# One attention-and-MLP decode kernel: w2 in five pieces, biases by one product each, and six unread products around the second norm

## The chip, the cores and the metric

The kernel runs on one core of one Trainium2 chip. The metric is the device time of one execution in microseconds (us). Lower is better. Three executions of the kernel before are at hand, and a fourth that was taken with the hardware profiler.

## What is computed

Eight tokens (B = 8, one position each, D = 512) go through one transformer block with modulation from a condition `c`. All numbers are float32.

```python
mod = (silu(c) @ w_mod).reshape(8, 6, 1, 512)
sa, ca, ga, sb, cb, gb = (mod[:, i] for i in range(6))
h = layernorm(x) * (1 + ca) + sa
x = x + ga * attention(h)          # 32 query heads, 8 cached heads, last 2048 of 8192 positions
h = layernorm(x) * (1 + cb) + sb
u = h @ w1 + b1                    # w1: 512 x 1792
x = x + gb * (relu(u) ** 2 @ w2 + b2)   # w2: 1792 x 512
```

The cached keys and values in the window and all weights are read from device memory once: 165 MB.

## The kernel before, in words

**Loads.** All large loads go out on SP's queue in the order of the list `loads`: `w_mod` and `wq` in two parts each, then keys and values of the eight tokens in turn, then `wo`, `w1` and `w2`. They share four buffers of 4 MB, `slot0` to `slot3`; `done()` frees a buffer behind its last reader and `pump()` issues the next load. `load()` (line 81) cuts the last ones into pieces, so that products can start on a piece while the next is on its way: `wo` in four, `w1` in three (two of its four row blocks, then one, then one), and `w2` like this:

```python
cuts = ((0, 8), (8, 11), (11, 12), (12, 13))
pieces = [(lo, v[:, lo:hi]) for lo, hi in cuts]
```

A unit of these cuts is one row of `w2` on each of 128 partitions, 256 KB, 13 in all (`FC`). The 128 rows of `w2` that are left over, the "extra" rows, go to the tile `w2x`, which lies in the memory of `qb_all`, in two small loads ahead of these (line 108). The tile framework gives each load on a hardware queue one of eight semaphores in turn, so a load also waits until the load eight places ahead of it has landed.

**Layout.** A row vector of 512 is spread over the partitions in four groups of 32, of which eight are in use, with 128 columns each. Most products have 32 columns of the array as target (`32 * q : 32 * q + 32`), and four of them stand side by side. In the profile a float32 product is two MATMUL records and two LDWEIGHTS records.

**The end of the program**, which the change touches, is a chain through all engines:

1. The attention's output times `wo` on PE (lines 472 to 497), then gate and residual on DVE (498, 499); the latter also leaves the row sums `x1sum`.
2. The second layer norm, `norm()` (line 170): PE sums `x1sum` over the groups with `sel` (line 173), DVE makes the mean, ACT squares the difference and sums it (line 178), PE sums that (line 182), ACT takes the root (184), DVE scales, shifts and transposes to `h2T` (188 to 192, 157).
3. `h2T` times `w1` on PE: the bias `b1` is put into the sum by products with a piece of the identity, one for each of four groups (line 509) and two for the extra columns (513); then for each of four row blocks `kc` two products for the extra columns into `px` (522) and four for the main columns into `ph` (530).
4. ACT takes the relu of `px` (539) and of `ph` in two halves (548, 551); DVE squares and transposes each to `rxT` and `rT` (549 to 554).
5. The product with `w2` on PE: four products for `b2` (558), then 17 chunks of four products (565): first the four of the extra rows (`rxT`, `w2x`), then the thirteen of the main rows (`rT`, `w2t`), in order. Each main chunk needs its piece of `w2`.
6. DVE applies gate and residual (573, 574), and SP stores the result.

PE works through its instructions in program order, and so do ACT and DVE.

Of the kernel before, what the change touches and what calls it, by code (L numbers as in the profile page):

```python
# [8 lines left out]
F32 = mybir.dt.float32  # L9
AF = mybir.ActivationFunctionType  # L10
# [8 lines left out]
def tile_adaln_cached_attention_mlp(  # L19
# [14 lines left out]
    nc = tc.nc  # L34
    P = 128
    B, HKV, SK, DH = k_cache.shape
    D = wq.shape[0]
# [27 lines left out]
    b1_x = consts.tile([1, FX], F32, name="b1_x")  # L65
    b2_in = consts.tile([NQ, P], F32, name="b2_in")
    nc.scalar.dma_start(b1_in, b1[: P * FC].rearrange("(g n) -> g n", g=NQ))
    nc.scalar.dma_start(b1_x, b1[P * FC :].rearrange("(g n) -> g n", g=1))
    nc.gpsimd.dma_start(b2_in, b2.rearrange("(g n) -> g n", g=NQ))


# [9 lines left out]
    def load(key):  # L81
        s = free.pop(0)
        t = slots[s]
        held[key] = s
        kind = key[0]
        if kind in "KV":

            src = k_cache if kind == "K" else v_cache
            v = src[key[1], 4 * key[2] : 4 * key[2] + 4, SK - W :, :]
            v = v.rearrange("x (i j) d -> i x (j d)", i=32)  # L90
            nc.sync.dma_start(t, v)
            return
        if kind == "mod":
            pieces = [(0, w_mod.rearrange(r_kc, p=P)[:, 2 * key[1] : 2 * key[1] + 2])]
        elif kind == "wq":
            pieces = [(0, wq.rearrange(r_kc, p=P)[:, 2 * key[1] : 2 * key[1] + 2])]
        elif kind == "wo":
            v = wo.rearrange("(p i) n -> p i n", p=P)
            cuts = ((0, 16),) if key[1] == 0 else ((16, 24), (24, 28), (28, 32))
            pieces = [(lo - 16 * key[1], v[:, lo:hi]) for lo, hi in cuts]  # L100
        elif kind == "w1":
            v = w1.rearrange(r_kc, p=P)
            pieces = [(lo, v[:, lo:hi]) for lo, hi in ((0, 2), (2, 3), (3, 4))]
        else:

            for g, o, first, _ in EXTRA:
                v = w2[first : first + 16 * o].rearrange("(i o c) n -> o i (c n)", i=4, o=o)
                nc.sync.dma_start(w2x[g : g + 4 * o, :], v)
            v = w2[: P * FC].rearrange("(p c) n -> p c n", p=P)
            cuts = ((0, 8), (8, 11), (11, 12), (12, 13))  # L110
            pieces = [(lo, v[:, lo:hi]) for lo, hi in cuts]
        for lo, v in pieces:
            a, n = v.shape[1:]
            nc.sync.dma_start(t[:, lo * n : (lo + a) * n].rearrange("p (a n) -> p a n", n=n), v)
# [52 lines left out]
    def bank(name="m_ps"):  # L167
        return ps_m.tile([P, 512], F32, name=name, tag="m_ps")

    def norm(xt, rowsum):  # L170

        pa = bank()
        nc.tensor.matmul(pa[:, 0:1], sel, rowsum, start=True, stop=True)  # L173
        nmean = work.tile([P, 1], F32, name="nmean")
        nc.vector.tensor_scalar(nmean, pa[:, 0:1], -1.0 / D, None, op0=ALU.mult)
        sq = work.tile([P, P], F32, name="sq", bufs=1)
        ssq = work.tile([P, 1], F32, name="ssq")
        nc.scalar.activation(sq, xt, AF.Square, bias=nmean, scale=1.0, accum_out=ssq)
        xm = work.tile([P, P], F32, name="xm", bufs=1)
        nc.vector.tensor_scalar(xm, xt, nmean, None, op0=ALU.add)  # L180
        pb = bank()
        nc.tensor.matmul(pb[:, 0:1], sel, ssq, start=True, stop=True)
        rstd = work.tile([P, 1], F32, name="rstd")
        nc.scalar.activation(rstd, pb[:, 0:1], AF.Sqrt, bias=eps, scale=1.0 / D)
        return xm, rstd
# [285 lines left out]
    for i in range(28):  # L471
        nc.tensor.matmul(  # L472
            wo_ps[32 * (i % 4) : 32 * (i % 4) + 32, :],
            oT[:, i, :],
            slot(("wo", i // 16), D)[:, i % 16, :],
            start=(i < 4),
            stop=(i >= 24),
        )
    x1 = consts.tile([P, P], F32, name="x1")
    x1sum = work.tile([P, 1], F32, name="x1sum")  # L480
    at_i = work.tile([P, D], F32, name="at_i", tag="a")
# [15 lines left out]
            )  # L497
    nc.vector.tensor_mul(x1, pw[:, :P], mods[0][:, 2, :])
    nc.vector.scalar_tensor_tensor(x1, x1, 1.0, x_in, op0=ALU.mult, op1=ALU.add, accum_out=x1sum)
    xm, rstd = norm(x1, x1sum)  # L500
    nc.vector.tensor_mul(xm, xm, mods[1][:, 1, :])
    h2T = scaled(xm, rstd, mods[1][:, 0, :], "h2T")

    w1t = slot(("w1",), F)
    w2t = slot(("w2",), D)
    ph = ps_t.tile([P, 512], F32, name="t_ps")
    px = bank()
    for g in range(NQ):
        nc.tensor.matmul(
            ph[32 * g : 32 * g + 32, :FG], one[:NQ, g : g + 1].to_broadcast([NQ, 32]), b1_in, start=True, stop=False  # L510
        )
    for g, o, _, at_ in EXTRA:
        nc.tensor.matmul(
            px[g : g + 32, : 16 * o],
            one[:1, :1].to_broadcast([1, 32]),
            b1_x[:, at_ : at_ + 16 * o],
            start=True,
            stop=False,
        )
    for kc in range(NQ):  # L520
        for g, o, first, _ in EXTRA:
            nc.tensor.matmul(
                px[g : g + 32, : 16 * o],
                h2T[:, kc, :],
                w1t[:, kc, first : first + 16 * o],
                start=False,
                stop=(kc == NQ - 1),
            )
        for g in range(NQ):
            nc.tensor.matmul(  # L530
                ph[32 * g : 32 * g + 32, :FG],
                h2T[:, kc, :],
                w1t[:, kc, g * FG : (g + 1) * FG],
                start=False,
                stop=(kc == NQ - 1),
            )

    for g, o, _, _ in EXTRA:
        nc.scalar.activation(
            rx[g : g + 32, : 4 * o, :].rearrange("p (o i) c -> p i o c", i=4),  # L540
            px[g : g + 32, : 16 * o].rearrange("p (i o c) -> p i o c", i=4, o=o),
            AF.Relu,
        )
    r = work.tile([P, 32, FC], F32, name="relu", tag="a")
    rT = work.tile([P, FC, 32], F32, name="rT", bufs=1)
    rxT = work.tile([64, 4, 32], F32, name="rxT", bufs=1)
    h = ph[:, :FG].rearrange("p (l c) -> p l c", l=32)
    nc.scalar.activation(r[:, :, :6], h[:, :, :6], AF.Relu)
    nc.vector.tensor_mul(rx, rx, rx)
    nc.vector.transpose(rxT, rx.rearrange("p l c -> p c l"))  # L550
    nc.scalar.activation(r[:, :, 6:], h[:, :, 6:], AF.Relu)
    for lo, hi in ((0, 6), (6, FC)):
        nc.vector.tensor_mul(r[:, :, lo:hi], r[:, :, lo:hi], r[:, :, lo:hi])
        nc.vector.transpose(rT[:, lo:hi], r[:, :, lo:hi].rearrange("p l c -> p c l"))

    py = ps_t.tile([P, 512], F32, name="t_ps")
    for q in range(NQ):
        nc.tensor.matmul(
            py[32 * q : 32 * q + 32, :P], one[:NQ, q : q + 1].to_broadcast([NQ, 32]), b2_in, start=True, stop=False
        )  # L560
    chunks = [(rxT[:, c, :], w2x[:64, D * c : D * c + D]) for c in range(4)]
    chunks += [(rT[:, f, :], w2t[:, f, :]) for f in range(FC)]
    for f, (left, right) in enumerate(chunks):
        for q in range(NQ):
            nc.tensor.matmul(  # L565
# [46 lines left out]
```

## Time and profile before

| | |
|---|---|
| three executions | 391.80, 391.89, 392.67 us; median 391.89 us |
| the profiled execution | 392.46 us, of which its span is 390.7 us |
| busy shares of the span | PE 66%, DVE 55%, PE's weight loads 30%, ACT 11%, GpSimd (POOL) 2% |
| moved by the DMA engines | 165.05 MB, mean 422 GB/s over the span |
| the chain that ended last | DMA 55%, DVE 24%, PE 20% of the span |

The profile is of one execution. Times in it are counted from the start of its span. "Granted clock" (PEclk) is the share of full speed that the chip granted to PE's clock: 1.0 is 2.4 GHz, 0.5 is 1.2 GHz. "DMA share" is the mean busy share of the 16 DMA engines; in short stretches it can read over 1.

### The profile page before, as it was taken

The page shows a single profiled execution, that of the slowest core. Times are in us where ns is not written, and L with a number is a line of the kernel's source. Part 1 is how long each engine was busy: PE and PEld are TensorE (multiplying, and loading weights), DVE is VectorE, ACT ScalarE, POOL GpSimd, SP SyncE. Part 2 cuts the span into 40 slices and gives each one's busy share as a digit, 9 for nine tenths or more (in the row PEclk, how much of TensorE's full clock was granted, in tenths as well). Part 3 has the DMA queues.
Part 4 walks back from the last instruction along what each step waited for, and adds up shares of the span by engine and source line. Part 5 has one row for each costly group of instructions (what it writes and reads, how often), then busy time and mean ns, then how long its engine had stood idle before and what let it go on. Part 6 is the DMA issues. An engine that isn't in the chain of part 4 may idle for free.

```text
span 390.7 us, 4952 instructions
## 1 busy us (share of the span) xinstructions
PE 257.5 (66%) x2196; PEld 116.3 (30%) x2196; DVE 214.3 (55%) x231; ACT 42.4 (11%) x90; POOL 6.1 (2%) x13
## 2 busy tenths in 40 slices
PE   0282808678966693859485939394849485984975
PEld 0120301151341342223322523143324323352344
DVE  3420299399394939284928491939293937330031
ACT  0310100030030003001200120003000300140010
POOL 4000000000000000000000000000000000100000
PEclk9997768969976998778688977786889777898788
DMA  8999999999999999999999999999999999999994
GB/s 325 435 429 434 436 429 450 433 439 429 428 429 428 429 428 429 429 438 440 429 433 431 436 441 433 429 431 429 428 429 429 435 433 428 433 438 414 428 427 166
DMA packets 7079, 165.05 MB, mean 422 GB/s; under 512 B 841, under 2 KB 1010, under 8 KB 1650
## 3 DMA queue, kind: packets, MB, share of 16 engines
q1 hardware_dynamic: 6952, 164.70, 98.1%
q8 instruction: 17, 0.28, 0.3%
q10 hardware_dynamic: 74, 0.04, 0.0%
q14 instruction: 4, 0.03, 0.0%
q0 software_dynamic: 32, 0.00, 0.0%
HBM read 164.67 MB, written 0.07 MB: 422 GB/s over the span
## 4 chain that ended last, share of the span: by engine, by line
DMA 55%; DVE 24%; PE 20%; issue 1%; ACT 0%; SPq 0%; DVEq 0%; ACTq 0%
DMA slot<-in_A_k_cache_dram 34%; DVE slot L304 22%; PE s_ps L314 16%; DMA slot<-in_A_wq_dram 7%; DMA slot<-in_A_wo_dram 6%; DMA slot<-in_B_w_dram 5%; DMA slot<-in_w_mod_dram 3%; PE t_ps L260 2%; PE t_ps L565 1%; PE m_ps L275 1%; PE t_ps L385 1%; DVE pT L386 0%; PE o_ps L397 0%; ACT qrep L283 0%; ACT prd L375 0%
## 5 line engine op out<-in xcount | busy, mean ns | idle before, releaser
L304 DVE STREAM_TRANSPOSE slot<-slot 128x2048 f32<-128x2048 f32 x64 | 143.8, 2282 | 41.7 <-DMA slot<-in_A_k_cache_dram 41.7
L314 PE MATMUL s_ps<-slot,qb_all 128*32 128x512 f32 x512 | 121.7, 1098 | 67.9 <-DVE slot L304 67.5
L314 PEld LDWEIGHTS s_ps<-slot,qb_all 128*32 128x32 f32 x512 | 22.6, 136 | 146.2 <-issue 80.8
L397 PE MATMUL o_ps<-slot,pT 128*32 128x256 f32 x1024 | 60.1, 382 | 0.5 <-DMA slot<-in_A_v_cache_dram 0.5
L397 PEld LDWEIGHTS o_ps<-slot,pT 128*32 128x32 f32 x1024 | 48.4, 112 | 26.5 <-issue 18.9
L385 PE MATMUL t_ps<-ident,prd 128*128 128x128 f32 x128 | 26.0, 358 | 17.3 <-ACT prd L375 9.6
L328 DVE STREAM_TRANSPOSE s<-s_ps 128x512 f32<-128x512 f32 x8 | 5.7, 717 | 54.6 <-PE s_ps L314 54.6
L385 PEld LDWEIGHTS t_ps<-ident,prd 128*128 128x128 f32 x128 | 19.0, 180 | 23.2 <-ACT prd L375 22.7
L375 ACT ACTIVATE prd<-pr,rz 128x512 f32<-128x512 f32 x32 | 20.5, 710 | 9.4 <-DVE rz L367 9.4
L351 ACT ACTIVATE pr<-s,nm 128x512 f32<-128x512 f32 x8 | 5.8, 722 | 140.9 <-DVE nm L345 140.9
L386 DVE TENSOR_TENSOR pT<-t_ps,m 128x512 f32<-128x512 f32 x32 | 20.2, 668 | 0.7 <-PE t_ps L385 0.6
L407 ACT COPY o_sb<-o_ps 128x256 f32<-128x256 f32 x16 | 5.8, 363 | 122.1 <-PE o_ps L397 122.1
L260 PE MATMUL t_ps<-slot,h1T 128*32 128x512 f32 x64 | 10.3, 799 | 8.4 <-DMA slot<-in_A_wq_dram 6.9
L472 PE MATMUL s_ps<-slot,oT 128*32 128x512 f32 x56 | 9.1, 816 | 5.0 <-DMA slot<-in_A_wo_dram 5.0
L173 PE MATMUL m_ps<-xsum,sel 128*128 128x1 f32 x2 | 0.6, 363 | 16.4 <-DVE xsum L196 16.4
L272 DVE STREAM_TRANSPOSE qT<-t_ps 128x512 f32<-128x512 f32 x2 | 1.4, 716 | 15.9 <-PE t_ps L260 15.9
L291 DVE TENSOR_TENSOR qb_all<-qrep,block 128x512 f32<-128x512 f32 x8 | 8.8, 1096 | 2.1 <-ACT qrep L283 2.1
L363 PE MATMUL m_ps<-z,same 128*128 128x1 f32 x16 | 3.2, 268 | 9.5 <-ACT pr L351 9.5
L238 PE MATMUL m_ps<-slot,cT 128*32 128x384 f32 x64 | 8.3, 695 | 0.0
L482 DVE COPY at_i<-s_ps 128x256 f32<-128x256 f32 x1 | 0.4, 426 | 13.3 <-PE s_ps L472 13.3
L322 POOL MEMSET qb_all<- 64x2048 f32 x1 | 1.8, 1801 | 332.3 <-PE s_ps L314 332.3
L260 PEld LDWEIGHTS t_ps<-slot,h1T 128*32 128x32 f32 x64 | 2.3, 137 | 15.8 <-DMA slot<-in_A_wq_dram 7.8
(105 smaller groups left out, 107.2 us busy)
## 6 DMA issues: line engine op xcount, KB each, us to landing
slot<-in_A_k_cache_dram SPq DMA_DIRECT2D x16, 4096.0 KB, 18.5
slot<-in_A_v_cache_dram SPq DMA_DIRECT2D x16, 4096.0 KB, 28.2
slot<-in_A_wq_dram SPq DMA_DIRECT2D x2, 4096.0 KB, 16.9
slot<-in_w_mod_dram SPq DMA_DIRECT2D x2, 3072.0 KB, 13.6
slot<-in_A_wo_dram SPq DMA_DIRECT2D x1, 4096.0 KB
slot<-in_A_wo_dram SPq DMA_DIRECT2D x1, 2048.0 KB
slot<-in_A_wo_dram SPq DMA_DIRECT2D x2, 1024.0 KB
slot<-in_B_w_dram SPq DMA_DIRECT2D x1, 2048.0 KB
```

What stands on the lines that cost most here:

```text
L238: nc.tensor.matmul(pm[i][32 * q : 32 * q + 32, : 3 * P].rearrange("p (m n) -> p m n", m=3), cT[:, kc, :], wm[:, 3 * i : 3 * i + 3, q, :], ...
L260: nc.tensor.matmul(pq[t][32 * x : 32 * x + 32, :], hT[:, kc, :], w[:, 2048 * t + 512 * x : 2048 * t + 512 * x + 512], start=(kc == 0), sto ...
L291: nc.vector.tensor_mul(qb[b % 2][:, :, :, :REP], qrep_b[:, :, None, :, b].to_broadcast([P, 32, 4, REP]), block[:, None, :, None].to_broadc ...
L304: nc.vector.transpose(k, k)
L314: nc.tensor.matmul(S_[b][32 * x : 32 * x + 32, :].rearrange("p (j i) -> p j i", i=8), q[:, n : n + 32], k[:, :, c, :, x], start=(t == 0 an ...
L351: nc.scalar.activation(pr.rearrange("p j (a i) -> p j a i", a=4), S2_.pop(b).rearrange("p (a j i) -> p j a i", a=4, i=8), AF.Exp, bias=NM_ ...
L375: nc.scalar.activation(d, pr[:, 4 * n : 4 * n + 4, :, None].to_broadcast([P, 4, 32, 4]), AF.Copy, scale=RZ_[b][0])
L385: nc.tensor.transpose(pp[:, P * i : P * i + P], d[:, i].rearrange("p i u -> p (i u)"), one)
L386: nc.vector.tensor_mul(PT_[b][:, n].rearrange("p q j (x r) -> p q (j x) r", r=REP), pp.rearrange("p (y q r) -> p q y r", y=16, r=REP), m16 ...
L397: nc.tensor.matmul(o[32 * (m % 4) : 32 * (m % 4) + 32].rearrange("p u d -> p (u d)"), PT_[b][:, n, 2 * q + t, 2 * u : 2 * u + 2, :].rearra ...
L407: nc.scalar.copy(O_[b][:, t], o)
L472: nc.tensor.matmul(wo_ps[32 * (i % 4) : 32 * (i % 4) + 32, :], oT[:, i, :], slot(("wo", i // 16), D)[:, i % 16, :], start=(i < 4), stop=(i ...
```

## The change

The biases `b1` (main columns) and `b2` come in by one product each, with the tile `fours` (128 columns, made by a copy on DVE) in place of four pieces of the identity. The extra columns of `w1` are taken with one product per row block, 64 columns of the array wide, from `h2d`, which is `h2T` twice; these come behind the products of the main columns. On ACT and DVE the main halves come first, and the extra columns stand between them or behind them. The main rows of `w2` come in five pieces instead of four, and the chunks of the extra rows stand behind the first four main chunks. `idle(n)` issues n products of the identity with itself, which nobody reads: two ahead of each of the norm's sums, and two behind the bias. The load of `b1_x` moves from ACT's queue to POOL's.

```diff
-    nc.scalar.dma_start(b1_x, b1[P * FC :].rearrange("(g n) -> g n", g=1))
+    nc.gpsimd.dma_start(b1_x, b1[P * FC :].rearrange("(g n) -> g n", g=1))
...
-            cuts = ((0, 8), (8, 11), (11, 12), (12, 13))
+            cuts = ((0, 4), (4, 8), (8, 11), (11, 12), (12, 13))
...
-    def norm(xt, rowsum):
+    def norm(xt, rowsum, idle=lambda n: None):
+        idle(2)
         pa = bank()
         nc.tensor.matmul(pa[:, 0:1], sel, rowsum, start=True, stop=True)
...
+        idle(2)
         pb = bank()
         nc.tensor.matmul(pb[:, 0:1], sel, ssq, start=True, stop=True)
...
+    fours = work.tile([NQ, NQ, 32], F32, name="fours", tag="prd", bufs=4)
+    nc.vector.tensor_copy(fours, one[:NQ, :NQ, None].to_broadcast([NQ, NQ, 32]))
+    four = fours.rearrange("k g b -> k (g b)")
...
-    xm, rstd = norm(x1, x1sum)
+    def idle(n):
+        for _ in range(n):
+            junk = ps_o.tile([P, 2, P], F32, name="o_ps")
+            nc.tensor.matmul(junk[:, 0, :], one, one, start=True, stop=True)
+
+    xm, rstd = norm(x1, x1sum, idle)
...
+    h2d = work.tile([P, NQ, 2, 32], F32, name="h2d", tag="prd", bufs=4)
+    nc.vector.tensor_copy(h2d, h2T[:, :, None, :].to_broadcast([P, NQ, 2, 32]))
...
-    for g in range(NQ):
-        nc.tensor.matmul(
-            ph[32 * g : 32 * g + 32, :FG], one[:NQ, g : g + 1].to_broadcast([NQ, 32]), b1_in, start=True, stop=False
-        )
-    for g, o, _, at_ in EXTRA:
-        nc.tensor.matmul(
-            px[g : g + 32, : 16 * o],
...
+    nc.tensor.matmul(ph[:, :FG], four, b1_in, start=True, stop=False)
+    idle(2)
     for kc in range(NQ):
-        for g, o, first, _ in EXTRA:
-            nc.tensor.matmul(
-                px[g : g + 32, : 16 * o],
...
+    nc.tensor.matmul(px[:64, :FX], one[:1, :1].to_broadcast([1, 64]), b1_x, start=True, stop=False)
+    for kc in range(NQ):
+        nc.tensor.matmul(
+            px[:64, :FX],
+            h2d[:, kc].rearrange("p a b -> p (a b)"),
+            w1t[:, kc, P * FC :],
...
-    nc.scalar.activation(r[:, :, :6], h[:, :, :6], AF.Relu)
-    nc.vector.tensor_mul(rx, rx, rx)
-    nc.vector.transpose(rxT, rx.rearrange("p l c -> p c l"))
-    nc.scalar.activation(r[:, :, 6:], h[:, :, 6:], AF.Relu)
-    for lo, hi in ((0, 6), (6, FC)):
+    halves = ((0, 6), (6, FC))
+    for lo, hi in halves:
+        nc.scalar.activation(r[:, :, lo:hi], h[:, :, lo:hi], AF.Relu)
+
+    for g, o, _, at_ in EXTRA:
+        nc.scalar.activation(
...
+    for lo, hi in halves:
         nc.vector.tensor_mul(r[:, :, lo:hi], r[:, :, lo:hi], r[:, :, lo:hi])
         nc.vector.transpose(rT[:, lo:hi], r[:, :, lo:hi].rearrange("p l c -> p c l"))
+        if lo == 0:
+            nc.vector.tensor_mul(rx, rx, rx)
+            nc.vector.transpose(rxT, rx.rearrange("p l c -> p c l"))
...
-    for q in range(NQ):
-        nc.tensor.matmul(
-            py[32 * q : 32 * q + 32, :P], one[:NQ, q : q + 1].to_broadcast([NQ, 32]), b2_in, start=True, stop=False
-        )
-    chunks = [(rxT[:, c, :], w2x[:64, D * c : D * c + D]) for c in range(4)]
-    chunks += [(rT[:, f, :], w2t[:, f, :]) for f in range(FC)]
+    nc.tensor.matmul(py[:, :P], four, b2_in, start=True, stop=False)
+    chunks = [(rT[:, f, :], w2t[:, f, :]) for f in range(FC)]
+    chunks[4:4] = [(rxT[:, c, :], w2x[:64, D * c : D * c + D]) for c in range(4)]
```

**Where it moves instructions.** Three places follow, first as they are before and then as they are changed. Rows give the line, the operation, what is written and read, the shape, and the semaphores waited for: `DMAHW3` is one of the eight of the hardware queues, `DMASW0` one of POOL's queue, and the others are engines. The second program's lines are a few higher for the same text.

The first place is PE between the last products with `wo` and the first with `w1` (`m_ps` of lines 173 and 182 are the norm's sums, `t_ps` is `ph`, the later `m_ps` is `px`, `o_ps` the target nobody reads, `slot_91` holds `w1`). Before:

```order
L173 MATMUL m_ps<-x1sum,sel 128x1 [waits DVE_49,PE_49]
L182 MATMUL m_ps<-ssq,sel 128x1 [waits PE_49,Activation_49]
L509 MATMUL t_ps<-b_in,ident 32x416 x4
L513 MATMUL m_ps<-b_x,ident 32x80 [waits DVE_49]
L513 MATMUL m_ps<-b_x,ident 32x48
L522 MATMUL m_ps<-slot_91,h2T 32x80 [waits DMAHW6_49,DVE_49]
L522 MATMUL m_ps<-slot_91,h2T 32x48
L530 MATMUL t_ps<-slot_91,h2T 32x416 x4
```

Changed:

```order
L510 MATMUL o_ps<-ident 128x128 [waits PE_49] x2
L174 MATMUL m_ps<-x1sum,sel 128x1 [waits DVE_49,PE_49]
L510 MATMUL o_ps<-ident 128x128 [waits PE_49] x2
L184 MATMUL m_ps<-ssq,sel 128x1 [waits Activation_49]
L522 MATMUL t_ps<-b_in,fours 128x416
L510 MATMUL o_ps<-ident 128x128 [waits PE_49] x2
L526 MATMUL t_ps<-slot_91,h2T 32x416 [waits DMAHW5_49,DVE_49]
L526 MATMUL t_ps<-slot_91,h2T 32x416 x7
```

Six products of 128x128 now stand ahead of instructions of the chain, each pair in front of one; two products per row block and five bias products are gone from here.

The second place is PE's product with `w2` (`rxT` and `qb_all` are the extra rows, `rT` and `slot_90` the main rows). Before:

```order
L565 MATMUL t_ps<-qb_all,rxT 32x128 [waits DMAHW1_49,DMAHW2_49,DVE_49,Pool_49]
L565 MATMUL t_ps<-qb_all,rxT 32x128 x15
L565 MATMUL t_ps<-slot_90,rT 32x128 [waits DMAHW3_49,DVE_49]
L565 MATMUL t_ps<-slot_90,rT 32x128 x23
L565 MATMUL t_ps<-slot_90,rT 32x128 [waits DVE_49]
```

Changed:

```order
L569 MATMUL t_ps<-slot_90,rT 32x128 [waits DMAHW2_49,DVE_49]
L569 MATMUL t_ps<-slot_90,rT 32x128 x15
L569 MATMUL t_ps<-qb_all,rxT 32x128 [waits DMAHW0_49,DMAHW1_49,DVE_49,Pool_49]
L569 MATMUL t_ps<-qb_all,rxT 32x128 x15
L569 MATMUL t_ps<-slot_90,rT 32x128 [waits DMAHW3_49]
```

Sixteen main products, on the first piece alone, moved ahead of the sixteen of the extra rows; the wait for the second piece comes behind both.

The third place is SP's queue at the end (128x4096 is a piece of 2 MB, 128x2048 one of 1 MB). Before:

```order
L108 DMA qb_all<-in_B_w_dram 12x1x2048 [waits DMAHW2_49]
L114 DMA slot_90<-in_B_w_dram 128x4096 [waits DMAHW3_49,PE_49]
L114 DMA slot_90<-in_B_w_dram 128x1536 [waits DMAHW4_49,PE_49]
L114 DMA slot_90<-in_B_w_dram 128x512 [waits DMAHW5_49,PE_49]
L114 DMA slot_90<-in_B_w_dram 128x512 [waits DMAHW6_49,PE_49]
L575 DMA out_dram<-y 128x128 [waits DMAHW7_49,DVE_49]
```

Changed:

```order
L108 DMA qb_all<-in_B_w_dram 12x1x2048 [waits DMAHW1_49]
L114 DMA slot_90<-in_B_w_dram 128x2048 [waits DMAHW2_49,PE_49]
L114 DMA slot_90<-in_B_w_dram 128x2048 [waits DMAHW3_49,PE_49]
L114 DMA slot_90<-in_B_w_dram 128x1536 [waits DMAHW4_49,PE_49]
L114 DMA slot_90<-in_B_w_dram 128x512 [waits DMAHW5_49,PE_49]
L114 DMA slot_90<-in_B_w_dram 128x512 [waits DMAHW6_49,PE_49]
L579 DMA out_dram<-y 128x128 [waits DMAHW7_49,DVE_49]
```

The semaphores of all loads but the last few moved down by one, since `b1_x` left the hardware queues; the three last pieces now each wait for a load that stands one place later than before.

## Rows read from the trace of the kernel before

**Rows 1.** The page's slices: rate of the DMA engines in 40 equal slices

```profile
GB/s 325 435 429 434 436 429 450 433 439 429 428 429 428 429 428 429 429 438 440 429 433 431 436 441 433 429 431 429 428 429 429 435 433 428 433 438 414 428 427 166
```

**Rows 2.** The end of the chain that ended last: start us, us, what

```profile
364.60 18.32 DMA slot<-in_B_w_dram
382.91 0.14 issue
383.05 4.53 PE t_ps L565 x104
...
387.60 0.30 DVE y L573
```

**Rows 3.** Stretches of the end: us, busy by engine (instructions), granted clock, DMA share, GB/s

```profile
364.60:369.40 4.80, 4.26 (x36) 1.03 (x28) 0.43 (x1) 0.01 (x1) 0.00 (x0) 0.90 1.02 435
...
372.40:374.70 2.30, 1.33 (x14) 0.67 (x14) 1.51 (x6) 0.76 (x3) 0.00 (x0) 1.00 0.98 413
...
375.90:379.10 3.20, 3.20 (x29) 1.77 (x25) 0.00 (x0) 0.00 (x0) 0.00 (x0) 0.50 1.05 442
379.30:382.60 3.30, 2.15 (x48) 0.99 (x40) 2.29 (x6) 1.02 (x4) 0.00 (x0) 1.00 0.96 403
382.70:385.60 2.90, 2.55 (x49) 2.58 (x53) 0.00 (x0) 0.00 (x0) 0.00 (x0) 0.50 0.76 302
385.60:386.00 0.40, 0.40 (x15) 0.40 (x8) 0.00 (x0) 0.00 (x0) 0.00 (x0) 0.50 0.02 5
386.10:387.50 1.40, 1.40 (x52) 1.17 (x44) 0.00 (x0) 0.00 (x0) 0.00 (x0) 1.00 0.00 0
```

**Rows 4.** Timeline around the second norm: start us, us, engine, line, what [idle before]

```profile
371.92 0.35 PE L173 MATMUL m_ps<-x1sum,sel 128*128 128x1 f32 x2 [0.82 <-DVE x L499]
...
373.05 0.38 PE L182 MATMUL m_ps<-ssq,sel 128*128 128x1 f32 x2 [0.78 <-ACT sq L178]
...
373.36 0.90 PE L509 MATMUL t_ps<-b_in,ident 4*32 4x416 f32 x8
...
374.35 0.40 DVE L157 STREAM_TRANSPOSE h2T<-h_sb 128x128 f32<-128x128 f32 x1
```

**Rows 5.** Timeline from the first product with w1 to the squares

```profile
374.80 0.26 PE L522 MATMUL m_ps<-slot,h2T 128*32 128x80 f32 x2 [0.42 <-DVE h2T L157]
...
376.97 0.54 PE L522 MATMUL m_ps<-slot,h2T 128*32 128x48 f32 x3
...
378.56 0.60 PE L522 MATMUL m_ps<-slot,h2T 128*32 128x48 f32 x3
...
379.08 0.94 PE L530 MATMUL t_ps<-slot,h2T 128*32 128x416 f32 x5
...
379.41 0.44 ACT L539 ACTIVATE rx<-m_ps 32x80 f32<-32x80 f32 x2 [5.68 <-PE m_ps L522]
379.88 0.28 DVE L549 TENSOR_TENSOR rx<-rx 64x128 f32<-64x128 f32 x1 [5.13 <-ACT rx L539]
...
380.11 0.35 ACT L548 ACTIVATE relu<-t_ps 128x192 f32<-128x192 f32 x1 [0.26 <-PE t_ps L530]
...
380.69 1.08 PE L565 MATMUL t_ps<-qb_all,rxT 64*32 64x128 f32 x32 [0.32 <-issue]
...
381.70 0.56 DVE L554 STREAM_TRANSPOSE rT<-relu 128x224 f32<-128x224 f32 x1
```

**Rows 6.** SP: timeline row of its last weight issues, and a wait after 364 us

```profile
364.60 9.49 SPq L114 DMA_DIRECT2D slot<-in_B_w_dram  x4
...
SPq L575 <- DMA slot<-in_B_w_dram: 1.7, 1, 1.7
```

**Rows 7.** Timeline: eight records of four products of 128x128 with the identity

```profile
344.71 1.24 PE L385 MATMUL t_ps<-ident,prd 128*128 128x128 f32 x8 [0.26 <-DVE pT L386]
```

**Rows 8.** Timeline of the start: POOL's issue of b2, and PE's first instruction

```profile
1.23 0.65 POOL L69 DMA_DIRECT2D b_in<-in_B_b_dram  x1 [0.79 <-POOLq L598]
...
16.41 0.59 PE L173 MATMUL m_ps<-xsum,sel 128*128 128x1 f32 x2 [16.41 <-DVE xsum L196]
```

More of the change, by code (lines that the diff above doesn't have):

```diff
@@ L507, in tile_adaln_cached_attention_mlp @@
     px = bank()
-    for g in range(NQ):
-        nc.tensor.matmul(
-            ph[32 * g : 32 * g + 32, :FG], one[:NQ, g : g + 1].to_broadcast([NQ, 32]), b1_in, start=True, stop=False
-        )
-    for g, o, _, at_ in EXTRA:
-        nc.tensor.matmul(
-            px[g : g + 32, : 16 * o],
[L515 to L518, printed above, removed]
-        )
-    for kc in range(NQ):
-        for g, o, first, _ in EXTRA:
-            nc.tensor.matmul(
-                px[g : g + 32, : 16 * o],
[L524 to L528, printed above, removed]
+    nc.tensor.matmul(ph[:, :FG], four, b1_in, start=True, stop=False)
+    idle(2)
+    for kc in range(NQ):
         for g in range(NQ):
@@ L536, in tile_adaln_cached_attention_mlp @@
             )
[L538 to L542, printed above, removed]
+    nc.tensor.matmul(px[:64, :FX], one[:1, :1].to_broadcast([1, 64]), b1_x, start=True, stop=False)
[4 more added lines that the diff above has]
+            w1t[:, kc, P * FC :],
+            start=False,
+            stop=(kc == NQ - 1),
         )
@@ L547, in tile_adaln_cached_attention_mlp @@
     h = ph[:, :FG].rearrange("p (l c) -> p l c", l=32)
-    nc.scalar.activation(r[:, :, :6], h[:, :, :6], AF.Relu)
-    nc.vector.tensor_mul(rx, rx, rx)
-    nc.vector.transpose(rxT, rx.rearrange("p l c -> p c l"))
-    nc.scalar.activation(r[:, :, 6:], h[:, :, 6:], AF.Relu)
-    for lo, hi in ((0, 6), (6, FC)):
+    halves = ((0, 6), (6, FC))
[3 more added lines that the diff above has]
+        nc.scalar.activation(
+            rx[g : g + 32, : 4 * o, :].rearrange("p (o i) c -> p i o c", i=4),
+            px[g : g + 32, at_ : at_ + 16 * o].rearrange("p (i o c) -> p i o c", i=4, o=o),
+            AF.Relu,
+        )
+    for lo, hi in halves:
         nc.vector.tensor_mul(r[:, :, lo:hi], r[:, :, lo:hi], r[:, :, lo:hi])
         nc.vector.transpose(rT[:, lo:hi], r[:, :, lo:hi].rearrange("p l c -> p c l"))
+        if lo == 0:
+            nc.vector.tensor_mul(rx, rx, rx)
+            nc.vector.transpose(rxT, rx.rearrange("p l c -> p c l"))
     py = ps_t.tile([P, 512], F32, name="t_ps")
-    for q in range(NQ):
-        nc.tensor.matmul(
-            py[32 * q : 32 * q + 32, :P], one[:NQ, q : q + 1].to_broadcast([NQ, 32]), b2_in, start=True, stop=False
-        )
-    chunks = [(rxT[:, c, :], w2x[:64, D * c : D * c + D]) for c in range(4)]
-    chunks += [(rT[:, f, :], w2t[:, f, :]) for f in range(FC)]
+    nc.tensor.matmul(py[:, :P], four, b2_in, start=True, stop=False)
+    chunks = [(rT[:, f, :], w2t[:, f, :]) for f in range(FC)]
+    chunks[4:4] = [(rxT[:, c, :], w2x[:64, D * c : D * c + D]) for c in range(4)]
     for f, (left, right) in enumerate(chunks):
```

## The prediction, made before the changed kernel was run

> **What bounds the kernel now.** I read the slices of the page first. The DMA engines move 428 to 450 GB/s in almost every slice and 166 in the last [rows 1]. So until some 382 us the time is the time of the bytes, which the change leaves alone, and only the tail can move. Then I read the end of the chain [rows 2]: the first piece of w2's main rows, 2 MB, is awaited until 382.91; PE begins at 383.05, works through all 104 records of the main chunks, and DVE takes the result at 387.60. The stretches of the end [rows 3] show two things. The DMA engines finish at about 385.6 (share 0.02 after that), so PE runs 2.0 us behind the last byte. And the granted clock of PE is 0.50 from 375.9 to 379.1, while the products with w1 run, and again from 382.7 to 386.0, while those with w2 run; it is 1.00 between and after. The timeline of the norm [rows 4] shows what came ahead of the first drop: short products with waits of 0.8 us between them, and bias products on four rows.
>
> Two prices come from this. A chunk of four products costs 0.27 us at the full clock: 1.08 us for the four chunks of the extra rows [rows 5]. At half it costs 0.40: of the 4.5 us for 13 chunks, the 1.5 us after 386.0 hold 5.6 chunks at 0.27, which leaves 7.4 for the 3.0 us before.
>
> **The change, part by part.**
>
> *The split piece.* With the first 1 MB as a piece of its own, PE can begin earlier. The whole 2 MB landed at 382.91; half of it at 403 GB/s [rows 3] takes 2.6 us, which gives 380.3. Forward: w1's second piece had landed at 364.60 + 9.49 + 1.7 = 375.8, the end of SP's issues and of its wait for that load [rows 6]; behind it come 0.92 MB of w1, 0.26 of extra rows and 1.05 of the new piece, 2.23 MB, at 442 then 403 GB/s: 381.1. I take 380.7. The second half lands at 382.91, as now. From there to 385.6, 1.31 MB land; by their sizes the third piece comes at 384.5, the fourth at 385.05, the last at 385.6, as before.
>
> One more load on SP's queue costs an issue of 0.3 us or so, and moves the last two pieces' waits by one load: the last one now waits for w1's second piece, 375.8 instead of 373.8. That is 9.8 us ahead of its landing, with over 3 MB queued before it, so I take nothing. Were the queue to run dry there, the cost would be a hole in the DMA share of 442 GB/s rows, which show none today with the same depth of eight.
>
> *w1 at the full clock.* The six products are to keep PE busy. One costs 1.24/4 = 0.31 us [rows 7], a pair 0.62 at the full clock, 1.24 at half. The first pair falls into the 0.82 us of waiting before the first sum, the second into the 0.78 before the second [rows 4]: hidden, with 0.2 us to spare. Behind the second sum, at 373.4, come the one bias product (at most the 0.90 of the four it replaces) and the third pair: 374.9, against 374.75 for `h2T`. So it may cost 0.1 to 0.2 us, bounded by 0 and 0.3. If the clock then stays at 1.0, a row block costs at most 0.90, three end by 377.7, and the fourth waits for w1's last piece, 0.92 MB after 375.8, at 377.9. `ph` is done at 378.8, where it is now 379.08 + 0.94 = 380.02 [rows 5].
>
> *The order behind it.* The first relu ends at 379.25, its square and transpose at about 380.15. The extra columns now come behind: five products at 0.31 at most, so 380.35, relu 0.44, then the four other DVE operations; all six take 2.38 us today (379.88 to 382.26 [rows 5]), so the last transpose ends at about 382.5. The wait that this adds, DVE's for the extra relu ahead of the second half, delays only chunks 6 to 12, which need 382.91 anyway. The two new copies on DVE fall where DVE waits for PE.
>
> *w2.* Bias 0.3, then chunks 0 to 3 at 380.85 behind the first piece, to 381.95; the extra rows to 383.05; chunks 4 to 7 from 383.05, behind the second piece; then 8 to 10, 11, and the last after 385.6 + 0.14, so PE ends at 386.05 at the full clock. With half the clock from 382.7, as now, nine chunks at 0.40 end at 386.6, or 386.45 if the clock rises at 386.0 again. Against 387.55 that is 1.5 or 1.1 us; I take **1.3 us**.
>
> *The start.* POOL issues one more load, 0.65 us [rows 8], and the identity comes that much later; PE first needs it at 16.41, some 11 us after it is ready. `wq`'s first part no longer waits for the eighth load before it; that queue held work all the time, so a gain or loss there is at most what the first slice's 325 GB/s hides, and I take 0.
>
> *The page that speaks against the cut.* The rows say that wo's two pieces of 1 MB, with runs as short as the new ones, and w1's of 0.92 MB moved at 435 and 442 GB/s [rows 3]. The Trainium skill (DMA: Bandwidth & Descriptors, Bandwidth) says that a load of 1 MB reaches 341 GB/s and one of 16 MB 425. By that page the 2 MB in two loads would take 6.2 us, an estimate from its figure, where the whole takes 5.2 by the rate of the rows; the trace disagrees with it here, since the loads queue behind each other.
>
> **Against which time.** The sum is made against the profiled execution: 392.46 - 1.3 = 391.16. That execution lies 0.57 above the median of the three, 391.89, and they spread over 0.87. If the median's runs have the same tail, the new median is 390.6. If their 0.57 is that they had the clock in w2 already (nine chunks at 0.13 less would be 1.2), the change has less to give and ends at the same 391.16, because the last byte sets it. I take the middle, **390.9**, a gain of 0.25%; the likeliest case by itself spans 390.3 to 391.2. About 0.2%, 0.8 us, is what a measurement of this kernel can tell from no change.
>
> **The rivals.**
>
> *The six products do not hold the clock* (chance 0.2). For it: the waits on both sides of the pairs remain, and PE was busy for 1.33 of 2.30 us there [rows 3] and the clock still fell. Against: 1.9 us of full 128x128 products are added. Then row blocks two to four cost up to 1.6 (376.97 to 378.56 with the extra columns in it [rows 5]), 1.35 without, `ph` ends near 379.5, the last transpose at 383.2, and nine chunks from 383.4 end near 386.7: 0.9 less, 391.0 to 391.55, mostly within the bound.
>
> *The first piece lands no earlier* (0.12). The 16 engines finish unevenly (share 0.76 at the end [rows 3]); if the last of them sets both halves, PE meets the wait for it at 382.9 with all 17 chunks behind it, the extra rows among them, whose 1.08 us now run under that wait. 383.05 + 17 x 0.27 = 387.65: no change, 391.9.
>
> *Smaller pieces move slower* (0.05). At the lowest full slice, 325 GB/s [rows 1], 2 MB cost 1.25 us more; the last byte comes at 386.85, PE ends at 387.2: 391.5. This is how the page named above would have it.
>
> *The six products stand in the way: slower* (0.06). If the granted clock is already 0.50 when PE meets them, the second pair delays the second sum by 0.45 us, and bias (1.8) and third pair (1.24) hold w1 back to 376.9. Four row blocks at 1.4 end at 382.5, five extra products at 0.62 at 385.6, the extra rows' transpose at 386.8, and 13 chunks follow: 389.5 or later, 2 us more, 393.9. It decides when the clock falls before 373.4; today it is 1.00 until 374.7 with less work, which speaks against it.
>
> **Chances.** The forecast has 0.57. Of it 0.05 falls within the bound, of the first rival 0.05 outside it; the second and third are within it but for 0.02; the last is slower, and 0.01 more for the spread. Faster by over 0.2%: 0.57, within 0.2%: 0.34, slower: 0.09. The range takes in the forecast, the first two rivals and the spread above the middle: 390.2 to 391.9.
>
> **What would show it.** Right: a granted clock of 1.00 from 375 to 379; `ph` done near 378.8; PE on chunks 0 to 3 before 382; PE's last chunk starting within 0.3 us of the last landing; DVE's gate near 386.2. Wrong: PE waiting until 382.9 for its first chunk; a clock of 0.50 under w1; DMA engines that finish later than 385.6; or an end that still trails the last byte by over 1 us.

## The result, and the profile after

The changed kernel takes **392.99 us** (median of 22 executions, 391.67 to 393.36); before, beside it on the same chips, takes 391.85 us (22 executions, 391.38 to 392.97). The ratio is 1.0022, with a 95% interval of 1.0015 to 1.003: it became slower by about 0.2%, where the forecast was 390.9 us and faster. The profiled execution took 392.98 us, of which its span is 391.1.

Before's 22 times lie in two groups, 13 from 391.38 to 391.92 and 9 from 392.67 to 392.97; the execution behind the rows ahead of the prediction, 392.46 us, is of the upper kind. Of the changed kernel's 22 times, 20 lie from 392.79 to 393.36, and two are lower (391.67 and 392.11).

Stretches of the end in the changed kernel; columns as in [rows 3] (PE, PE's weight loads, DVE, ACT, POOL, granted clock, DMA share, GB/s):

```profile
372.40:374.70 2.30, 2.07 (x11) 1.27 (x12) 1.38 (x6) 0.76 (x3) 0.00 (x0) 1.00 1.03 432
375.10:379.10 4.00, 3.20 (x34) 0.88 (x33) 0.21 (x1) 0.00 (x0) 0.00 (x0) 1.00 1.02 426
379.30:382.60 3.30, 3.30 (x71) 2.67 (x72) 2.33 (x6) 0.92 (x4) 0.00 (x0) 1.00 1.01 423
382.70:385.60 2.90, 1.97 (x68) 1.42 (x59) 0.00 (x0) 0.00 (x0) 0.00 (x0) 1.00 0.78 311
385.60:387.50 1.90, 0.48 (x20) 0.19 (x8) 0.00 (x0) 0.00 (x0) 0.00 (x0) 1.00 0.03 9
```

The clock is 1.00 in every one of them, and the loads move 423 to 432 GB/s until the last ones run out. Then read the last row: from 385.6 to 387.5 the DMA engines are almost idle (share 0.03), and so is PE, 0.48 us busy out of 1.90. The timeline says what for, first through the norm and w1, then through w2:

```profile
372.36 0.69 PE L510 MATMUL o_ps<-ident 128*128 128x128 f32 x4
...
373.59 0.96 PE L522 MATMUL t_ps<-b_in,fours 4*128 4x416 f32 x2
...
374.48 0.71 PE L510 MATMUL o_ps<-ident 128*128 128x128 f32 x4
374.58 0.41 DVE L157 STREAM_TRANSPOSE h2T<-h_sb 128x128 f32<-128x128 f32 x1
...
375.12 2.30 PE L526 MATMUL t_ps<-slot,h2T 128*32 128x416 f32 x24
...
378.22 0.91 PE L526 MATMUL t_ps<-slot,h2T 128*32 128x416 f32 x8 [0.80 <-DMA slot<-in_B_w_dram]
...
382.12 0.58 DVE L558 STREAM_TRANSPOSE rT<-relu 128x224 f32<-128x224 f32 x1
```

```profile
380.44 0.48 PE L564 MATMUL t_ps<-b_in,fours 4*128 4x128 f32 x2
...
380.85 1.08 PE L569 MATMUL t_ps<-slot,rT 128*32 128x128 f32 x32
...
381.91 1.08 PE L569 MATMUL t_ps<-qb_all,rxT 64*32 64x128 f32 x32
...
383.09 1.08 PE L569 MATMUL t_ps<-slot,rT 128*32 128x128 f32 x32
...
385.00 1.08 PE L569 MATMUL t_ps<-slot,rT 128*32 128x128 f32 x32 [0.83 <-DMA slot<-in_B_w_dram]
...
387.54 0.42 PE L569 MATMUL t_ps<-slot,rT 128*32 128x128 f32 x8 [1.46 <-DMA slot<-in_B_w_dram]
388.03 0.29 DVE L577 TENSOR_TENSOR y<-t_ps,mod 128x128 f32<-128x128 f32 x1 [5.34 <-PE t_ps L569]
```

PE takes the chunks as the forecast had them, and then waits 1.46 us for the last 256 KB of w2. The chain that ended last says the same; its row of 104 records at the end [rows 2] is one of 8 now, behind a transfer that lasts from its issue at 376.10 to 387.49:

```profile
376.10 11.39 DMA slot<-in_B_w_dram
387.49 0.04 issue
387.54 0.47 PE t_ps L569 x8
388.01 0.02 issue
388.03 0.30 DVE y L577
```

**Who is late.** A load has landed when every DMA engine that carries part of it has reported. The trace has these 16 reports one by one (not part of the page). For w2's last piece, in us, the first five and the last three:

```
before  382.78 382.83 383.03 384.56 385.36 ... 385.96 385.98 386.06
after   382.90 382.92 383.24 384.67 385.44 ... 386.17 386.19 387.49
```

Fifteen engines finish much as in before, at 386.19 at the latest; one comes 1.30 us behind. The last four packets that end before that landing (start, end, bytes, queue) tell why. The trace doesn't number the engines; that the four are of one engine is read from their times, since each starts as the one before it ends:

```
385.473 386.395 16384 q8
386.381 386.612  2048 q1
386.597 386.824  2048 q1
386.810 386.835     4 q1
```

Each engine carries eight packets of 2048 bytes of that piece, and a record of 4 bytes behind them. On this one six have gone when a packet of 16 KB on another queue gets in and takes 0.92 us; the last two follow it, and at 0.23 us each, where the others take 0.08. The page lists that queue as one of instructions:

```profile
q1 hardware_dynamic: 7096, 164.70, 98.1%
q8 instruction: 17, 0.28, 0.3%
```

There are 17 such packets in before as well. The changed kernel has 2 x 2186 records of products and weight loads on PE (before 2 x 2196, so the change adds none on balance), 61 of PE's waits and the like, and 503 on the other four engines together, so I take them for fetches of PE's program, one per some 260 records. Two more facts of the traces speak for it: the 8th, 9th and 11th of them start behind record 1989, 2238 and 2724 of PE in both kernels; and in runs told below that add PE instructions early, the second one comes earlier (at 87.8 us in the changed kernel, 72.8 with 64 instructions more, 64.9 with 128 more). Before's last one runs from 385.44 to 386.38, but no packet of w2 starts behind it: a 4-byte record, the end of an engine's share, ends within 10 ns of the fetch's start. So nobody waits for it. The Trainium skill (DMA: Bandwidth & Descriptors, Queues, rings and completion order) says that an engine takes turns between its queues and drains a whole packet, typically 9 to 17 descriptors, before it switches. That before's fetch starts at the end of a share of nine records agrees. In the changed kernel the fetch starts with two of eight left, so the turn comes before a share of nine is drained there; whether a packet in the page's sense ends at that place, the trace doesn't show.

### The profile page after: what moved, and what is told of

Same layout as the page of the kernel before. It is cut to its first block, busy times and chain, and to the rows that moved or that the text cites. A ratio compares the mean times of both kernels' runs of the same rounds, so it can differ in the third digit from the quotient of the medians.

```text
span 391.1 us, 4936 instructions
## 1 busy us (share of the span) xinstructions
PE 257.1 (66%) x2186; PEld 116.9 (30%) x2186; DVE 215.3 (55%) x233; ACT 42.5 (11%) x90; POOL 6.6 (2%) x14
## 4 chain that ended last, share of the span: by engine, by line
DMA 55%; DVE 23%; PE 20%; ACT 1%; issue 1%; ACTq 0%; DVEq 0%; SPq 0%
DMA slot<-in_A_k_cache_dram 42%; DVE slot L306 20%; PE s_ps L316 16%; DMA slot<-in_B_w_dram 10%; DMA xc_in<-in_xc_dram 3%; PE m_ps L240 2%; PE t_ps L387 1%; PE o_ps L399 1%; DVE pT L388 1%; ACT prd L377 0%; DVE s L330 0%; DVE s L334 0%; DVE mx L339 0%; ACT L161 0%; ACTq L63 0%
## 5 line engine op out<-in xcount | busy, mean ns | idle before, releaser
L387 PE MATMUL t_ps<-ident,prd 128*128 128x128 f32 x128 | 27.3, 373 | 16.9 <-ACT prd L377 9.7
L387 PEld LDWEIGHTS t_ps<-ident,prd 128*128 128x128 f32 x128 | 20.4, 191 | 22.4 <-ACT prd L377 22.1
L425 DVE TENSOR_TENSOR og<-m_ps,m 128x128 f32<-128x128 f32 x8 | 2.2, 272 | 8.6 <-PE m_ps L417 8.6
```

The lines of the kernel that those rows point to most:

```text
L387: nc.tensor.transpose(pp[:, P * i : P * i + P], d[:, i].rearrange("p i u -> p (i u)"), one)
```

## The experiments

Twelve runs follow, in three lots of four, each lot on a chip of its own; each is compared with before on the same chip. The first four ask whether the fetch is the cause, and whether the unread products do anything. In this lot 16 of before's 35 times lie from 391.37 to 391.72 and 19 from 392.46 to 393.03, so a ratio a little under 1 means that a kernel lacks the upper group, not that it is faster than the lower one.

**Fewer PE instructions: one, then three gathers less.** The last fetch should move relative to the data, with the tail as it is. The first leaves the gather of the first token out, the second (with `b > 4` in the same place) those of the first three, so their outputs miss these tokens' attention.

```diff
-        if b > 1:
+        if b > 2:
             gather(b - 2)
```

> The changed kernel without the gather of the first token (its four products, 16 instructions of PE, and two DVE operations, some 280 us before the end; the first token's attention is left out). Fetch theory: the 1.3 us between the 15th and the 16th engine's landing of w2's last piece come from the last 16 KB instruction fetch (queue 8, at 385.47 for 0.92 us), which one DMA engine serves ahead of its last two packets; PE's count of instructions decides when that fetch is asked for. With 16 less it is asked for about one chunk later, behind PE's last wait for a piece: the last piece lands near 386.2 and the time is 391.7. Cut theory: the last piece lands late because it is issued at 376.1 behind one more piece; nothing here changes that: 392.9.

> The changed kernel without the gathers of the first three tokens (48 instructions of PE less, far before the end; those tokens' attention is left out). Fetch theory: the program now ends before the instruction that asks for the seventeenth fetch, or asks for it behind the last landing: 16 fetches or a harmless one, last piece at 386.2, 391.7 us. Cut theory: 392.9.

Measured: 391.71 us (391.48 to 392.03) and 391.60 us (391.32 to 391.78), 12 executions each, all below the 20 of the changed kernel; ratios to before 0.9988 (0.9978 to 0.9999) and 0.9984 (0.9973 to 0.9994). The end of the first one's chain:

```profile
375.82 10.26 DMA slot<-in_B_w_dram
...
386.13 0.47 PE t_ps L569 x8
```

The piece lands at 386.08, with all 16 engines within the old spread; the fetch runs 385.53 to 386.46, and no packet of w2 stands behind it. With three gathers less the piece lands at 386.21, and there are still 17 fetches, the last from 385.82: not their number changed but where the last one falls. Both expectations have it asked for later; in the first run it starts 0.06 us later than in the changed kernel (385.47), so what differs is whether its engine has packets left, not the time. The gathers left out save little of the time ahead of the tail: w2's second piece lands at 382.97 and 382.98 here, at 383.05 in the changed kernel. So nearly all of the 1.3 us are the collision's.

**More PE instructions: 16 unread products early.** These stand between the products with wq, 300 us ahead of the tail.

```diff
+        if kc == 2:
+            for _ in range(16):
+                junk = ps_o.tile([P, 2, P], F32, name="o_ps")
+                nc.tensor.matmul(junk[:, 0, :], one, one, start=True, stop=True)
```

> The changed kernel with 16 more unread products (64 instructions of PE) early, while PE waits for wq. Fetch theory: the last fetch is asked for some four chunks earlier, while more packets of its DMA engine are still to come; if an engine's packets simply queue behind each other, that engine ends as late as now: 392.9, with the last landing near 387.4. If only a fetch among the last packets hurts: 391.7. Cut theory: 392.9 in any case.

Measured: 392.86 us (391.52 to 393.36, 12 executions), ratio 1.001 (0.9997 to 1.0023): nine near 393, three at 391.5 to 391.8. In its profile the fetch (385.08 to 386.02) has six packets behind it, and the last engine reports at 387.39, the fifteenth at 386.16. This run also shows that the six products in the norm don't always hold the clock, though they are all there:

```profile
373.90:377.30 3.40, 3.40 (x24) 1.19 (x26) 0.47 (x2) 0.00 (x0) 0.00 (x0) 0.50 1.03 433
```

**No unread products.**

```diff
-        for _ in range(n):
+        for _ in range(0):
```

> The changed kernel without its six unread products (24 instructions of PE less). Fetch theory: the last fetch comes later, behind the last wait, so the last piece lands near 386.2; but the granted clock may fall to 0.50 under w1 or w2 again: PE ends between 386.6 and 387.2, 391.6 to 392.3. Cut theory: last landing near 387.5, and 392.9 or more.

Measured: **391.58 us** (391.50 to 391.73, 12 executions), ratio 0.9988 (0.9978 to 0.9998). Its last fetch starts at 385.39, not later as expected, with no packet of w2 behind it, and the last piece lands at 386.08. Its clock is half under w1, and PE still meets the data:

```profile
373.40:376.70 3.30, 3.00 (x17) 0.80 (x20) 0.95 (x3) 0.00 (x0) 0.00 (x0) 0.50 1.01 426
```

```profile
380.73 1.08 PE L569 MATMUL t_ps<-slot,rT 128*32 128x128 f32 x32
381.74 1.08 PE L569 MATMUL t_ps<-qb_all,rxT 64*32 64x128 f32 x32
383.08 1.08 PE L569 MATMUL t_ps<-slot,rT 128*32 128x128 f32 x32 [0.27 <-DMA slot<-in_B_w_dram]
384.90 1.65 PE L569 MATMUL t_ps<-slot,rT 128*32 128x128 f32 x40 [0.73 <-DMA slot<-in_B_w_dram]
```

So the unread products bring nothing that shows in the time: with or without them PE begins w2 at 380.7 to 380.9, and waits 0.7 to 0.8 us for the third piece. This kernel computes everything, and its 12 times are the narrowest of all.

**What before's two groups are.** Two more looks at before, and before with three gathers less (its first three tokens' attention is left out, as above).

> The kernel before, without the gathers of the first three tokens (48 instructions of PE less, far before the end; their attention is left out). The runs of the kernel before fall into two groups, 391.4 to 391.9 and 392.7 to 393.0. If the upper group is the instruction fetch in front of the last packets of one DMA engine (fetch theory), it goes: all runs at 391.4 to 391.9. If the upper group is the half clock under w2 (clock theory), it stays, some 4 of 10 runs at 392.7 or more.

> The kernel before, unchanged, for a second profile of it. Fetch theory: the profile shows either a last landing within 0.2 us of the 15th engine's and a time under 392.5, or one more than 1 us behind it and a time of 392.7 or more. Clock theory: the time goes with the granted clock under w2 alone, last landing near 386.1 in both.

> The same again, a third profile of the kernel before: fetch theory and clock theory as in the second.

With fewer gathers before still has both groups (seven at 391.36 to 391.59, five at 392.40 to 392.81; ratio 0.9999, 0.9987 to 1.0012), which speaks against fetches as what makes them; the profile behind the rows, of the upper kind, has no collision either (last report at 386.06). The three profiles took 391.46, 391.50 and 391.46 us, all of the lower kind. The second look:

```profile
374.30:377.60 3.30, 3.30 (x31) 1.78 (x29) 0.00 (x0) 0.00 (x0) 0.00 (x0) 0.50 1.06 441
...
382.70:386.00 3.30, 2.85 (x96) 2.47 (x96) 0.00 (x0) 0.00 (x0) 0.00 (x0) 1.00 0.66 263
```

```profile
383.03 2.85 PE L565 MATMUL t_ps<-slot,rT 128*32 128x128 f32 x96 [1.90 <-DMA slot<-in_B_w_dram]
386.08 0.43 PE L565 MATMUL t_ps<-slot,rT 128*32 128x128 f32 x8 [0.20 <-DMA slot<-in_B_w_dram]
```

Here the clock is full under w2, where it was half in [rows 3]. Twelve chunks take 2.85 us, PE waits 0.20 us for the last byte, and ends as the kernel without unread products does. So **before's lower runs are bound by the last landing already**; the split has about 1 us to give against the upper ones alone. That the clock under w2 makes the groups rests on one profile of the upper kind and three of the lower, one of them with gathers left out.

**The split undone.** The changed kernel with before's four pieces, and the chunks in the changed order.

```diff
-            cuts = ((0, 4), (4, 8), (8, 11), (11, 12), (12, 13))
+            cuts = ((0, 8), (8, 11), (11, 12), (12, 13))
```

> The changed kernel with w2's main rows in four pieces as before, all else as changed. The split's worth by my forecast: without it PE meets its wait at 382.9 with all 17 chunks behind it, 4.6 us at the full clock, so PE ends at 387.6 and the time is near 392.5, whatever the last landing does. If the split is worth nothing, because the last landing sets the end either way: 391.6 without a collision, 392.9 with one.

Measured: 394.49 us (6 executions: three at 393.88 to 394.07, three at 394.91 to 395.15), ratio 1.0056 (1.0038 to 1.0074). The profile is of 395.06 us.

```profile
382.30:389.00 6.70, 5.94 (x108) 4.90 (x112) 0.00 (x0) 0.00 (x0) 0.00 (x0) 0.50 0.38 149
```

```profile
383.06 1.94 PE L569 MATMUL t_ps<-slot,rT 128*32 128x128 f32 x32 [2.51 <-DMA slot<-in_B_w_dram]
384.93 1.93 PE L569 MATMUL t_ps<-qb_all,rxT 64*32 64x128 f32 x32
386.78 3.26 PE L569 MATMUL t_ps<-slot,rT 128*32 128x128 f32 x72
```

All 17 chunks stand behind the 2 MB, the extra rows among them, and behind a wait of 2.51 us the clock is half until 389: four chunks cost 1.94 instead of 1.08. The last piece lands at 386.03, with no fetch ahead of its packets. With this order the four pieces are 1.5 us slower than the changed kernel with its collision (394.49 against 392.99), and 2.9 us slower than the five pieces without one (391.58, where the unread products are gone too); the three stem from different lots. The 392.5 expected had the chunks at the full clock.

**Count or place.** Two runs of the last lot put the count and the tail apart. The first kernel has no unread products in the tail and six between those with wq, so as many PE instructions as the changed kernel; the second is the changed kernel with 32 there (both edits as above).

> The changed kernel with its six unread products issued between the products with wq instead of in the tail: PE's number of instructions up to w1 is that of the changed kernel, the tail is that of the kernel without unread products. Theory: PE's last instruction fetch stands at the same count, so it again falls between the last packets of w2, the last landing comes near 387.4 and the time near 392.9. Rival: what removed the collision in the kernel without unread products was their absence from the tail, not the count: last landing 386.1, time 391.6.

> The changed kernel with 32 unread products more between the products with wq, 128 PE instructions, half of the distance between two fetches. Theory: if fetches stand at fixed counts of PE's instructions, the last one falls some 128 instructions earlier or later than now, so ahead of the last packets or not at all; the last landing comes at 386.1 and the time at 391.6. Rival: the fetch's moment is set by something else (by when PE is let go, or by the queue) and stays at 385.4: then 391.6 or 392.9 by which packets it meets.

The first: 392.87 us (391.46 to 393.21, 10 executions), ratio 1.0007 (0.9992 to 1.0022), six near 393 and four at 391.5 to 391.8; in its profile, of 393.21 us, the fetch (385.58 to 386.54) has one packet behind it, and the last engine reports at 387.57, the fifteenth at 386.25.

```profile
375.88 11.69 DMA slot<-in_B_w_dram
...
387.62 0.70 PE t_ps L573 x8
```

So the collision is back without a single unread product in the tail; their absence there was not what removed it. The second: 393.23 us (392.84 to 393.79, 10 executions), ratio 1.0033 (1.0021 to 1.0044). The fetch did move, to 384.03 to 384.96, but one engine is late with the fourth and the fifth piece: 386.50 and 387.12, where the fifteenth reports at 385.52 and 386.13. Its last packet ends 1.77 us behind the fetch, the time of 16 packets of which the first few are slow, so the fetch stands in front of both pieces there.

```profile
376.04 11.07 DMA slot<-in_B_w_dram
...
387.16 0.47 PE t_ps L573 x8
```

My expectation that an earlier fetch is harmless falls: it is harmless only on an engine that has nothing left.

**The extra rows cut evenly.** The kernel without unread products, with

```diff
-    EXTRA = ((0, 5, P * FC, 0), (32, 3, P * FC + 80, 80))
+    EXTRA = ((0, 4, P * FC, 0), (32, 4, P * FC + 64, 64))
```

> The changed kernel without unread products, with the extra rows of w2 cut 4 and 4 instead of 5 and 3, so that both small loads have 16 rows of 8 KB. If the last landing is set by engines that carry a row more of these loads, it comes up to 0.3 us earlier than 386.1 and the time is 391.3; if not, 391.6 as without this. Should a fetch meet the last packets, 392.9.

Measured: 392.79 us (392.68 to 392.96, 10 executions), ratio 1.0021 (1.001 to 1.0031). It was slower by 1.2 us, and not by a fetch. The reports of the two small loads and of the last piece:

```
5 and 3:  376.08 376.13 376.42 376.83 378.00   377.34 377.34 377.64          ... 386.03 386.08
4 and 4:  376.31 376.37 376.87 377.87          377.56 377.59 378.09 379.12   ... 386.13 387.15
```

Loads of 20 and 12 rows are carried by five and three engines, loads of 16 and 16 by four and four. The Trainium skill (DMA: Bandwidth & Descriptors, Why a DMA increments its semaphore by 16 and not by 1) says that the number is the largest up to 16 that divides the slowest dimension of both sides (here 5 and 20, 3 and 12, 4 and 16: so 5, 3 and 4), and that the lowest-numbered engines are taken; the numbers of reports agree, and which engines they are the trace doesn't show. If the same engines take both loads, then evenly cut a fourth one, behind the others already (378.00 in the first line, 377.87 in the second), carries 32 KB more. One engine's report stays 1.0 us behind in every later piece, to 387.15.

**Split and order alone, in before.**

```diff
-            cuts = ((0, 8), (8, 11), (11, 12), (12, 13))
+            cuts = ((0, 4), (4, 8), (8, 11), (11, 12), (12, 13))
...
-    chunks = [(rxT[:, c, :], w2x[:64, D * c : D * c + D]) for c in range(4)]
-    chunks += [(rT[:, f, :], w2t[:, f, :]) for f in range(FC)]
+    chunks = [(rT[:, f, :], w2t[:, f, :]) for f in range(FC)]
+    chunks[4:4] = [(rxT[:, c, :], w2x[:64, D * c : D * c + D]) for c in range(4)]
```

> The kernel before with two parts of the change alone: w2's main rows in five pieces and the first four main chunks ahead of the extra rows. Biases, clock and the order on ACT and DVE are before's. Theory: the tail then ends with the last landing at either clock, or at most 0.3 later: chunks 0 to 3 from about 382.3, extra rows to 384.4 at the worst, nine chunks at 0.40 to 388.0 at half the clock, 387.0 where the clock rises at 386. So 391.6 in runs at the full clock under w2, where before has 391.5 too, and 391.9 to 392.4 otherwise, where before has 392.4 to 393. Rival: the fetch meets the last packets here too, since the count of PE's instructions differs little: 392.9 in most runs.

Measured: 391.89 us (12 executions: eight at 391.70 to 391.95, four at 393.04 to 393.43), ratio 1.0005 (0.9991 to 1.0019). Its profile, of 391.70 us, ends with the data:

```profile
384.87 1.08 PE L565 MATMUL t_ps<-slot,rT 128*32 128x128 f32 x32 [0.78 <-DMA slot<-in_B_w_dram]
386.14 0.42 PE L565 MATMUL t_ps<-slot,rT 128*32 128x128 f32 x8 [0.19 <-DMA slot<-in_B_w_dram]
```

None of its times lies in the upper group of before in this lot (392.39 to 392.97), but four are above it, where colliding runs lie; none of the four was profiled, so that they are collisions is argued, not shown. By its median this kernel, too, is no faster than before.

## Why the prediction was wrong

- *The split piece*: right for the two megabytes. The first megabyte landed at 380.60 (forecast 380.7), the second at 383.05 (382.91), the third and fourth at 384.95 and 385.58 (384.5 and 385.05).
- **The step that failed is "the last at 385.6, as before".** It landed at 387.49, 1.9 us later. 1.3 us of that come from a PE instruction fetch on one of 16 DMA engines, in front of that engine's last two packets: I counted the time of the new instructions on PE, and had no term for where PE's program is fetched among the data's packets. The page shows the queue in one row of 0.3%, which I passed over.
- The same step had a second, smaller error. I read 385.6 from a DMA share that fell to 0.02 [rows 3], a mean over 16 engines. By the reports before's last piece landed at 386.06, 0.3 us behind its last packet (385.74). That is also why the third and fourth pieces came 0.5 us behind the forecast. So the best end was 386.05 + 0.05 + 0.47 = 386.6 rather than 386.05, and the best time the 391.6 that was measured without the collision, not 390.9.
- *w1 at the full clock*: happened in the profiled run (1.00 from 372.4 on), and the third pair cost about 0.1 us as forecast: the first product with w1 starts at 375.12, `h2T` is done at 374.99. But it was worth nothing: `ph` was done at 379.13 (forecast 378.8) instead of 380.02 [rows 5], and PE came to chunk 0 at 380.85, 0.25 us behind the landing of its piece, only to wait 0.83 us for the third piece. The kernel without unread products, at half the clock under w1, waits 0.73 us there and takes 391.58 us.
- *The order behind it and w2*: right. The last transpose ends at 382.70 (382.5), chunks 0 to 3 start at 380.85 (380.85), the extra rows at 381.91 (381.95), chunks 4 to 7 at 383.09 (383.05).
- *The price of a chunk*: a little off, and without effect on the end. In before, chunks at half the clock start 0.42 us apart, in the kernel with four pieces 0.47, where I had 0.40; at the full clock 12 chunks took 2.85 us in the second look, 0.24 each, where I had 0.27.
- *The later issue of the last piece*: nothing, as forecast. The kernel without unread products issues it at 375.78 and has it at 386.08.
- *Against which time*: of my two readings, the second holds. Before's median lay in the group that has the full clock under w2, and there was nothing to take from it; I took the middle of both.
- *The rivals*: the first piece did land earlier; smaller pieces did not move slower (423 to 432 GB/s while they were on their way); the products did not stand in the way, though the sign of that rival is the one that came. That the clock isn't held did happen, in the run with 16 products early, and cost nothing that shows. The rival that came true, another transfer ahead of the last bytes, was not among them.

What stays open: what fixes the moment at which the fetch is let in between packets. Over the profiles its start lies between 384.03 and 386.13, and the PE records ahead of it vary from 4273 to 4477, in three profiles of before itself from 4342 to 4428. The 4273 are those of the kernel with four pieces, where the DMA engines had nothing else left to move; the changed kernel, with as many PE records, is past that record at 382.56, and its fetch starts at 385.47. If both ask for it at the same place, the fetch waits some 3 us for its turn in the changed kernel; no run settles that. With 16, 24 or 48 instructions less no execution of 36 was above 392.03 us; adding 64 did not end the collision, and 128 moved it in front of the fourth piece.

## What to carry to other kernels

When the end of a kernel is the landing of its last load, look at who finishes that load: the slowest of 16 DMA engines sets it, and a mean share hides that engine. Instruction fetches travel on the same engines, so instructions added only to keep an engine busy can cost time on the data's path: here, with 24 of them left out, no packet stood behind the last fetch, and the time was 391.58 us against 392.99, the best version that computes everything. It is not their number as such: before has more PE records than the changed kernel, and in none of its profiles a packet stands behind the last fetch. And a single profiled run of a kernel whose times lie in two groups shows one group: find out which, before taking a gain from it.

## What was not expected of the hardware

- One 16 KB fetch of PE's program occupies a DMA engine for 0.92 us, 17 times in this kernel. In the tail nothing evens it out: in the four profiles with a collision the engine ends 1.0 to 1.3 us behind the fifteenth.
- The 16 engines are far apart at the end anyway: for the same 256 KB the first reports at 382.78 and the last at 386.06 in before. A load of 12 or 20 long rows goes through three or five engines, and 32 KB more on one of them was 1.0 us later at the end.
- The first packets behind a fetch (up to three) took 0.23 us each instead of 0.08, and in three of these profiles the report came 0.4 to 0.8 us behind the last packet instead of 0.3, so the delay there (1.2 to 1.3 us) was longer than the fetch.
